# A kernel of windowed attention and a mixing MLP: its scheduler's order replaced by a written-out order, with loads and stores on two queues

## The chip, the cores and the metric

The kernel runs on one core of one Trainium2 chip. A core has five engines with a queue of instructions each: TensorE (PE, matmuls), ScalarE (ACT, activations and copies), VectorE (DVE, elementwise work), GpSimd (POOL, elementwise work and DMAs that cast) and SyncE (SP, which here issues DMAs and computes nothing). An engine takes its instructions in the order in which they stand; an instruction that has to wait for another engine waits on a semaphore, and what stands behind it waits with it. The metric is the time of the kernel on the device in microseconds (us).

## The reference

Attention over 4 batches, 8 heads, 768 positions and a head dimension of 64, in which a query sees the 128 positions up to its own and the first 4 positions (the sinks); then a block that mixes positions and channels.

```python
scores = scale * np.matmul(q, k.transpose(0, 1, 3, 2))
scores = np.where(is_sink | in_window, scores, -1000000000.0)
a = softmax(scores)                      # over keys
x = (a @ v) as [4, 768, 512]             # heads side by side
a1 = alpha1 * x + beta1
tok = np.einsum('ts,bsd->btd', w_tok, a1)
u = x + lam * tok
a2 = alpha2 * u + beta2
ch = np.maximum(a2 @ w_ch1, 0.0) @ w_ch2 # 512 -> 2048 -> 512
return u + lam * ch
```

All inputs and the output are float32.

## The kernel before

A batch goes through these steps, with tiles of 128 positions (six to a batch) and fp16 operands for TensorE:

- q and k of a pair of heads are loaded (`load_qk`, buffers `nat`), cast to fp16, transposed and put into `qkT`. In batch 0 most of them are cast by the DMA that GpSimd issues. In batches 0 and 1 TensorE transposes (`tp` tiles, L611 and L614), and ScalarE or VectorE copies the result from PSUM. In batches 2 and 3 (`b >= XB`, `XB = 2`) the DMA transposes, issued by SyncE (L630).
- `S` (L724, for some tiles with a mask bias at L719): scores of one tile of keys; ScalarE takes the exponent (`ex`, L746); VectorE or GpSimd masks the result (`mk`); `sk` and `vsp` do the sinks. `pv` (L825) multiplies with v; VectorE normalizes it into `x` (`norm`, L851). v comes by `load_v` and is cast into `vfs`.
- `xh` is the half-precision operand of the mixing: `lam * alpha1 * x` plus a constant, on GpSimd (`mul`, L869) and VectorE or GpSimd (`plus`, L872). `tok` (L956) multiplies it with the transposed w_tok; VectorE adds it to `x` (`ua`, L963), and the sum is cast to fp16 (`uc`, tile `u16`).
- `u16` is transposed into `uT`, in two halves of 384 positions: in batch 0 by TensorE (`uTp`, L997) with a scaled copy from PSUM, in the others by a DMA that SyncE issues (`uTx`, L1015) with a scaling in place (L980 on ScalarE, L982 on VectorE).
- `h` (L1036) is the first layer of the MLP, 16 tiles for each half, each four matmuls of 384 columns, and a ReLU on ScalarE or VectorE (L1042, L1044). The second layer is `ch` (L1221) in batch 0, and in batches 1 to 3 a two-level scheme with seven products instead of eight, `P1` to `P7` (L1153), with sums of halves on VectorE. The results are added to `x` and stored (`store`, L1172, and L1235).
- Weights come in early: w_tok by `load_wtok`, the four quarters of w_ch1 by DMAs on GpSimd that cast (`load_w1`), w_ch2 by `load_w` with a multiply by lam (L938).

No step is written down in the order in which it runs. Each is a task, added with `plan.add(prio, engs, fn, after, uses, ...)`: a priority, the engines that may run it and a cost in ns for each, the function that emits the instructions, the tasks it needs, the buffers it uses. There are 1,143 tasks. `Plan.run` (L132) then plays the kernel through with these costs, with a model of two DMA rings (`Rings`, L37) and fixed delays until an engine sees another's result (`SEEN`): at each step it takes the task that can start first, the higher priority first where two could start together, on the engine that would end it first, gives it free buffers, and so produces the order of every queue, the engine of every task and the buffer of every tile. The priorities come from the formulas of the code, changed at random by a list of 30 seeds (`TURNS`, L417, `shuffle`, L264). Where the model sees TensorE idle in the first 36 us it puts in matmuls on zeros (L349)[...].

All DMAs of loads and stores and all transposing DMAs are issued by SyncE; GpSimd issues those that cast, and ScalarE five small loads of parameters at the start. `gate` (L560) reads a few bytes of a quarter of w_ch1, so that SyncE waits at that point until the quarter is there. PSUM has four buffers of one bank (`d`, for everything but the scores) and two of two banks (`S`). `nat` has 8 buffers, `vnat` 4, `wst` 4, `hT` 2, `uT` and `qkT` one each.

The softmax here doesn't subtract the row's maximum and nothing guards it: scores larger than these inputs give would overflow.

## Time and profile before

| | |
|---|---|
| median of 3 runs | 257.1 us (256.68 to 257.15) |
| the profiled execution's own time | 257.06 us |
| its span, first to last instruction | 255.3 us |
| busy TensorE / VectorE / ScalarE / GpSimd | 247.4 / 190.0 / 142.6 / 88.3 us |
| HBM read, written | 29.91 MB, 6.29 MB |
| DMAs issued by SyncE for loads and stores | 101, and 34 that transpose |

The span is what the profile shows between the first and the last instruction; the execution's own time holds 1.8 us more around it. A busy TensorE is not a TensorE at its peak: matmuls are pipelined, a waiting matmul's row may be stretched, and the fillers on zeros count as busy. To see whether TensorE waits, one has to look at the steps between the starts of its matmuls. A group of the profile is named by its line; the lines of helpers (L356 is `nc.scalar.copy` in `copy`, L358 the same for the other engines) gather several tasks.

The largest loads' and stores' rows, with the median us from issue to landing:

```profile
out_dram<-x SPq DMA_DIRECT2D x21, 256.0 KB, 2.8
nat<-in_q_dram SPq DMA_DIRECT2D x13, 384.0 KB, 5.3
nat<-in_k_dram SPq DMA_DIRECT2D x13, 384.0 KB, 5.7
vnat<-in_v_dram SPq DMA_DIRECT2D x18, 256.0 KB, 5.2
```

The DMA engines are busy nearly throughout the first 70 us, and little after 170 us.

### The profile page before, as it was taken

Reading aid. Unit: us, or ns where it says so; the run is one execution under the profiler, and the core shown is the slowest. Engines: PE = TensorE matmul, PEld = TensorE weight load, DVE = VectorE, ACT = ScalarE, POOL = GpSimd, SP = SyncE. Lnnn points to the kernel's source line nnn. Section 1 sums busy time; section 2 is a strip of 40 time slices with the busy share of each in tenths; the row PEclk is TensorE's granted clock in tenths of the full one; section 3 lists DMA queues with packets and bytes.
Section 4 is the critical chain, followed back from the end, with each engine's and each line's share of the span. In section 5 each row is a group of like instructions: output and inputs, shape, how many; then the busy total and the mean of one; then the engine's idle time right before and its main releaser. Section 6 shows DMA issues by size and latency. Waiting matters only on the chain.

```text
span 255.3 us, 5519 instructions
## 1 busy us (share of the span) xinstructions
PE 247.4 (97%) x2174; PEld 160.9 (63%) x2174; DVE 190.0 (74%) x402; ACT 142.6 (56%) x236; POOL 88.3 (35%) x108
## 2 busy tenths in 40 slices
PE   8999998999999999899999999999999999999994
PEld 7754645675555544456678676558668666667883
DVE  6777998696878878578889997877789764136782
ACT  2689845989848035688971225867571125775000
POOL 7409802344445330159653460735310101000000
PEclk9999999999999999999999999999999999999999
DMA  6998999999943998599778689501000156000105
GB/s 202 195 223 292 216 230 392 373 370 218 218 73 115 186 260 190 117 205 220 155 138 182 125 191 251 85 3 21 3 0 3 59 167 146 0 0 3 63 4 185
DMA packets 86130, 38.80 MB, mean 152 GB/s; under 512 B 73540, under 2 KB 80460, under 8 KB 86104
## 3 DMA queue, kind: packets, MB, share of 16 engines
q1 hardware_dynamic: 82320, 35.14, 56.5%
q0 software_dynamic: 3744, 3.28, 8.1%
q8 instruction: 17, 0.28, 0.5%
q14 instruction: 9, 0.07, 0.1%
q10 hardware_dynamic: 40, 0.03, 0.0%
HBM read 29.91 MB, written 6.29 MB: 142 GB/s over the span
## 4 chain that ended last, share of the span: by engine, by line
PE 88%; DMA 4%; DVE 3%; POOL 1%; issue 1%; ACT 1%; POOLq 0%; ACTq 0%
PE h L1036 33%; PE P L1153 21%; PE tok L956 11%; PE ch L1221 8%; PE pv L825 5%; PE S L724 4%; DMA n<-in_q_dram 4%; DVE uT L982 1%; PE S L719 1%; PE tp L614 1%; PE pv L818 1%; POOL n L497 1%; PE wT L916 1%; ACT uT L980 1%; DVE w2f L1068 1%
## 5 line engine op out<-in xcount | busy, mean ns | idle before, releaser
L1036 PE MATMUL h<-uT,w1f 128*128 128x384 f16 x512 | 91.9, 326 | 2.7 <-DVE uT L982 1.3
L1036 PEld LDWEIGHTS <-w1f 128*128 128x128 f16 x512 | 47.3, 98 | 34.5 <-issue 5.5
L1042 ACT ACTIVATE hT<-h 128x384 f16<-128x384 f32 x99 | 48.3, 492 | 26.1 <-PE h L1036 25.6
L1153 PEld LDWEIGHTS <-hT 128*128 128x128 f16 x408 | 39.8, 98 | 6.7
L746 ACT ACTIVATE E<-S 128x1024 f16<-128x1024 f32 (+1 forms) x39 | 37.9, 1001 | 7.5 <-PE S L724 3.7
L869 POOL TENSOR_TENSOR tm<-x,la_b 128x512 f32<-128x512 f32 x18 | 26.2, 1454 | 26.3 <-DVE xh L872 19.1
L956 PE MATMUL tok<-xh,wtokT 128*128 128x512 f16 x144 | 33.4, 379 | 0.0
L356 ACT CAST u<-x 128x512 f16<-128x512 f32 x19 | 11.7, 618 | 31.2 <-DVE x L963 31.1
L1153 PE MATMUL P<-w2f,hT 128*128 128x256 f16 x216 | 25.9, 273 | 0.0
L1166 DVE TENSOR_TENSOR x<-x,P 128x256 f32<-128x256 f32 x45 | 18.3, 418 | 8.2 <-PE P L1153 7.9
L1044 DVE TENSOR_SCALAR hT<-h 128x384 f16<-128x384 f32 x29 | 15.8, 553 | 10.9 <-PE h L1036 10.5
L956 PEld LDWEIGHTS <-wtokT 128*128 128x128 f16 x144 | 14.0, 98 | 14.6
L1221 PE MATMUL ch<-w2f,hT 128*128 128x512 f16 x96 | 23.0, 379 | 0.0
L1153 PE MATMUL P<-w2s,hT 128*128 128x256 f16 x192 | 22.8, 273 | 0.0
L851 DVE TENSOR_TENSOR x<-pv,rec 128x256 f32<-128x256 f32 x48 | 20.4, 424 | 1.7
L358 POOL CAST vfs<-vnat 128x512 f16<-128x512 f32 x18 | 15.0, 840 | 16.2 <-DMA vnat<-in_v_dram 16.0
L963 DVE TENSOR_TENSOR x<-x,tok 128x512 f32<-128x512 f32 x24 | 16.2, 684 | 5.7 <-PE tok L956 5.7
L356 ACT CAST n<-nat 128x768 f16<-128x768 f32 x16 | 13.2, 829 | 10.8 <-DMA nat<-in_q_dram 8.8
L825 PEld LDWEIGHTS <-E 128*128 128x128 f16 x328 | 15.2, 97 | 6.0 <-issue 1.6
L825 PE MATMUL pv<-vfs,E 128*128 128x65 f16 x328 | 17.9, 194 | 0.0
L358 POOL CAST u<-x 128x512 f16<-128x512 f32 x5 | 3.1, 621 | 34.8 <-DVE x L963 21.1
L1221 PEld LDWEIGHTS <-hT 128*128 128x128 f16 x96 | 8.6, 98 | 9.1 <-issue 0.2
(131 smaller groups left out, 327.4 us busy)
## 6 DMA issues: line engine op xcount, KB each, us to landing
out_dram<-x SPq DMA_DIRECT2D x21, 256.0 KB, 2.8
nat<-in_q_dram SPq DMA_DIRECT2D x13, 384.0 KB, 5.3
nat<-in_k_dram SPq DMA_DIRECT2D x13, 384.0 KB, 5.7
vnat<-in_v_dram SPq DMA_DIRECT2D x18, 256.0 KB, 5.2
wst_w<-in_moe_w_ch_dram SPq DMA_DIRECT2D x8, 512.0 KB, 7.4
wtn<-in_moe_w_tok_dram SPq DMA_DIRECT2D x6, 384.0 KB, 4.7
w1f<-in_moe_w_ch_dram POOLq DMA_DIRECT2D x4, 512.0 KB, 11.1
v<-in_v_dram SPq DMA_DIRECT2D x12, 128.0 KB, 6.4
```

Of the source, the lines that this page charges most:

```text
L356: nc.scalar.copy(o, i)
L358: engine[e].tensor_copy(o, i)
L746: nc.scalar.activation(eT.t, pS.t[:, :, 0 : n * w].rearrange("p e (i w) -> p e i w", i=n), AF.Exp, scale=scale)
L825: nc.tensor.matmul(po.t[:, hl, :], eT.t[:, e_, off + i, c : c + P], vf[j][:, h, :], start=(r < 2 and n == 0), stop=(n == len(parts) - 1 an ...
L851: nc.vector.tensor_mul(bx.t[:, 4 * G : 4 * G + 4, :], po.t[:, :, 0:D], rec.t.to_broadcast([P, 4, D]))
L869: engine[e].tensor_mul(bt.t, bx.t.rearrange("p h d -> p (h d)"), la1_b)
L956: nc.tensor.matmul(pt.t, wtokT[:, si, ti * P : (ti + 1) * P], hs[si].t, start=(si == 0), stop=(si == NR - 1))
L1036: nc.tensor.matmul(ph.t, w1f[:, c, fi * P : (fi + 1) * P], bu.t[:, c, chk * NTOK : (chk + 1) * NTOK], start=(c == 0), stop=(c == NC - 1))
L1042: nc.scalar.activation(bh.t[:, fi, :], ph.t, AF.Relu)
L1153: nc.tensor.matmul(pc.t, hh[:, nt * P : (nt + 1) * P], w(fi), start=(first and n_ == 0), stop=(n_ == HF - 1), skip_group_check=True)
L1166: nc.vector.tensor_add(row(bx)[:, cols], row(bx)[:, cols], pc.t)
L1221: nc.tensor.matmul(pc.t, bh.t[:, fi, nt * P : (nt + 1) * P], w2f[:, fi, :], start=(fi == 0), stop=(fi == NF - 1))
```

## The change

The priorities, the model and the seeds go. Four literals take their place: `ORDER` (the 1,143 task numbers in the order in which they are emitted), `ENGINES` (one digit for each task: 0 ScalarE, 1 VectorE, 2 TensorE, 3 GpSimd, 4 SyncE), `HOMES` (one hexadecimal digit for each tile: its buffer) and `IDLES` (where the matmuls on zeros stand, in which PSUM buffer and how many: 101 of them, 106 before). `emit` goes through them. The tasks, what they need and what they compute are the same; the costs and priorities that are still handed to `add` are no longer read.

Loads of q, k and v of batches 1 to 3, of w_tok and w_ch2, and the stores may now be issued by ScalarE too: 25 of the 135 DMAs that were SyncE's are, 8 of q or k, 9 of v and 8 stores. The transposing DMAs stay on SyncE. `gates` has a tile of its own instead of a place in a `pt` buffer.

In number of tasks, VectorE has 336 (330 before), ScalarE 230 (229), GpSimd 108 (90), SyncE 110 (135), TensorE 359 as before. Of the 128 ReLUs, ScalarE has 81 (99 before) and VectorE 47 (29); of the 24 casts to `u16`, ScalarE 13 (19) and GpSimd 11 (5); of the 16 scalings of w_ch2, VectorE 11 (15) and GpSimd 5 (1).

```diff
-    def run(self, prio):
...
-    def emit(self, turns):
-
-        prio = [t.prio for t in self.tasks]
-        for seed in turns:
-            prio = shuffle(prio, seed)
-        for t, e, start, stop, idle in self.run(prio):
-            t.at = (e, start, stop)
+    def emit(self, order, engines, homes, idles):
+
+        own = iter(homes)
+        for t in self.tasks:
             for b in t.uses:
                 if b.home is None:
+                    b.home = int(next(own), 16)
+        fills = {i: (home, n) for i, home, n in idles}
+        for i in order:
+            t = self.tasks[i]
+            e = (ACT, DVE, PE, POOL, SP)[int(engines[i])]
+            idle = fills.get(i)
             if idle:
...
+    queue = {SP: nc.sync, ACT: nc.scalar}
...
-    gates = sb.tile([1, 32], FP16, tag="pt_1", bufs=1, name="gates")
+    gates = const.tile([1, 32], FP16, name="gates")
...
-    TURNS = (13523, 134113, 50022, 128275, 136711, 187603, 125671, 100730, 14946, 163131, 178432, 158827, 183776, 137680, 153375, 26742, 367527, 307353, 376563, 212018, 255075, 397706, 218147, 375675, 393913, 224567, 207692, 352780, 243076, 346008)
+    ORDER = (
+        26, 6, 0, 7, 9, 11, 10, 8, 18, 15, 1, 19, 45, 12, 46, 16, 47, 14, 72, 5, 48, 24, 2, 39, 49,
...
+    ENGINES = (
+        "3313134433443333444444444444444433334443131211201202021212021213030121210211201210210200"
...
+    HOMES = (
+        "5140061573001022031122213301312013300330310000011004121511643150013120133092018513113050"
...
+    IDLES = (
+        (46, 0, 54), (49, 0, 30), (90, 0, 3), (61, 3, 5), (68, 0, 2), (111, 3, 1), (88, 0, 2),
+        (166, 0, 4),
+    )
...
             done["nat", b, hp, t] = add(
-                p, {SP: 700}, lambda e: nc.sync.dma_start(
-                    bf.t.rearrange("p e (r d) -> p (e r) d", r=NR), src), [wait], [bf], lands=(96, 19.0))
+                p, {SP: 630, ACT: 600}, lambda e: queue[e].dma_start(
+                    bf.t.rearrange("p e (r d) -> p (e r) d", r=NR), src), [wait], [bf], lands=(96, 15.7))
...
         done["vn", b, r] = add(
-            p, {SP: 550}, lambda e: nc.sync.dma_start(
+            p, {SP: 570, ACT: 560}, lambda e: queue[e].dma_start(
...
         def store(p, bx, ti, cols, after):
             n_ = (cols.stop - cols.start) // 64
-            add(p, {SP: 480}, lambda e: nc.sync.dma_start(out[b, ti * P : (ti + 1) * P, cols], row(bx)[:, cols]),
+            add(p, {SP: 520, ACT: 550}, lambda e: queue[e].dma_start(out[b, ti * P : (ti + 1) * P, cols], row(bx)[:, cols]),
                 after, [bx], lands=(8, 12 * n_ if n_ == 8 else 60))
...
-    plan.emit(TURNS)
+    plan.emit(ORDER, ENGINES, HOMES, IDLES)
```

In the order of TensorE, with each run of tasks of one kind written once, the places that the prediction speaks of read as follows (`h0_0` is the first half of batch 0, `ch3` tile 3 of batch 0, a number behind x the tasks in a row):

```
before   tok0x7 uTp0x2 h0_0x4 uTp0x1 h0_0x1 uTp0x1 h0_0x4 ...
after    tok0x6 uTp0x2 tok0x1 h0_0x8 uTp0x2 h0_0x2 h0_1x9 ...

before   vsp2 ch5x2 tok1x3 ch5 tok1x3 h1_0x3 S2 sk2 h1_0x4 ...
after    vsp2 ch4 ch3 tok1x4 S2 tok1x1 ch4 ch3 tok1x1 S2 sk2 h1_0x7 ...
```

On GpSimd the start changes from `sel`, two DMAs, the identity, three DMAs, masks, `bm`, a DMA to the identity, three DMAs, masks, two DMAs, `sel`, a multiply of the parameters, `bm`, a DMA, another multiply.

## The prediction, made before the changed kernel ran

> **What bounds the kernel now.** I read the page's first two parts, then the chain of waits, then busy time by stretch, then the timeline around the two places where TensorE is short.
>
> ```profile
> span 255.3 us, 5519 instructions
> ...
> PE 247.4 (97%) x2174; PEld 160.9 (63%) x2174; DVE 190.0 (74%) x402; ACT 142.6 (56%) x236; POOL 88.3 (35%) x108
> ...
> PEclk9999999999999999999999999999999999999999
> ...
> PE 88%; DMA 4%; DVE 3%; POOL 1%; issue 1%; ACT 1%; POOLq 0%; ACTq 0%
> ```
>
> TensorE is busy 97% of the span at full clock, and the chain is TensorE for 88%. Both kernels give it the same matmuls, so only its waits can go. I sized them from the matmuls' start times: from the first matmul of a group to the first of the next, less the usual step of that kind: 0.650 us for a group of 4 in L1036 (`h`), 0.873 for 8 in L1153, 0.864 for 4 in L1221, 1.295 for 6 in L956 (`tok`), 0.24 to 0.54 for the small ones. The usual steps add up to 228.9 us. The other 26.4 lie as follows: 7.8 us up to 10 us (much of it before any input can be there), 6.3 from 10 to 30, 1.8 at 38.8 to 41.4, 2.0 at 98 to 104, 4.0 in small pieces (1.0 from 60 to 80, 1.0 from 110 to 130, 1.7 from 150 to 180 among them), nothing from 183 on, and some 4.4 after the last matmul's start.
>
> ```profile
> 0.00:17.00 17.00, 15.17 (x201) 11.41 (x201) 12.02 (x38) 9.11 (x14) 7.75 (x21) 1.00 1.04 205
> 17.00:30.40 13.40, 13.40 (x194) 7.88 (x194) 10.75 (x32) 13.08 (x22) 11.50 (x16) 1.00 1.01 253
> ...
> 38.50:42.00 3.50, 2.39 (x20) 1.39 (x19) 2.92 (x5) 2.01 (x4) 1.83 (x2) 1.00 1.06 406
> ...
> 98.00:104.00 6.00, 4.83 (x23) 2.07 (x22) 5.04 (x11) 3.06 (x5) 0.64 (x1) 1.00 0.83 179
> ```
>
> The columns are width, then PE, PEld, DVE, ACT, POOL busy with counts, clock, DMA share, GB/s. From 17 to 30.4 ScalarE is busy 13.08 of 13.40: it sets the pace there, and had 9.11 us of work done by 17. The two short rows are waits of matmuls, whose causes the timeline shows:
>
> ```profile
> 39.06 0.67 ACT L980 ACTIVATE uT<-uTp,ab 128x384 f16<-128x384 f16 x1 [1.04 <-PE uTp L997]
> ...
> 39.76 0.86 DVE L982 TENSOR_SCALAR uT<-uTp,ab 128x384 f16<-128x384 f16 x2 [0.40 <-ACT uT L980]
> ...
> 40.66 0.67 ACT L980 ACTIVATE uT<-uTp,ab 128x384 f16<-128x384 f16 x1 [0.93 <-DVE uT L982]
> ...
> 41.38 0.81 PE L1036 MATMUL h<-uT,w1f 128*128 128x384 f16 x4 [0.38 <-ACT uT L980]
> ```
>
> ```profile
> 95.97 4.02 SPq L1015 DMA_TRANSPOSE uT<-u  x3
> ...
> 101.80 0.70 ACT L980 ACTIVATE uT<-uT,ab 128x384 f16<-128x384 f16 x1
> ...
> 102.40 1.24 DVE L982 TENSOR_SCALAR uT<-uT,ab 128x384 f16<-128x384 f16 x3
> ...
> 102.83 1.35 PE L1036 MATMUL h<-uT,w1f 128*128 128x384 f16 x5 [1.07 <-DVE uT L982]
> ```
>
> In both, `h` waits for `uT`, and TensorE's order holds nothing else to fill the wait.
>
> **What the Trainium skill says.** "DMA: Bandwidth & Descriptors", section "Issuing engines are not separate DMA queues": transfers from all engines end on the same 16 DMA engines, and a second issuing engine saves only the sequencer's issue time. So I give the second queue no bandwidth. The trace has next to nothing on ScalarE's queue (40 packets), so it can't say. Section "Rules for kernel authors" of that page: two transposing streams must be kept apart, while a transpose beside ordinary DMAs needs nothing; all transposes stay on SyncE here, and I price no loss between them. "SBUF — State Buffer", section "SBUF: two separate sides": VectorE and GpSimd share a port pair that one holds for a whole instruction. The trace agrees: VectorE's scaling of w2 (L938), 0.69 us in the median, took 1.46 us at 41.13 beside GpSimd's 1.27 us multiply begun at 40.77.
>
> **The change part by part.** I call w the TensorE work, in us of the usual steps, that stands ahead of a task in an order.
>
> *Start.* Before, VectorE first casts w_tok (4.11), and the first cast of q begins at 6.39; ScalarE's first copy to `qkT` begins at 8.07. After, VectorE's first task is q's cast, and w_tok's goes to ScalarE. By the landing times of such loads (3.8 us at least from 1.27), the cast can start near 5.1 (0.76 long), six transposes follow (0.5), and ScalarE starts near 6.4, 1.7 earlier. But the last cast-on-load of k is issued by GpSimd near 9, as before (8.80), because the masks, `sel`, `bm` and a 1.2 us multiply stand ahead of it; it landed 8.2 us after issue, so near 17.1 both orders meet the same wall. Before, TensorE then had w = 5.9 behind it, after, 6.45. ScalarE's work ahead of `tok` (w = 16) is 24.9 us before and 25.2 after, by row durations. ScalarE's instructions overlap by 0.10, so of the 1.7 some 1.2 us counts at most, and the extra work and the wall take part of it. I take `tok` at 29.7 instead of 30.5: −0.8 (bounds −1.8 and +0.5).
>
> *First `uT` of batch 0.* After, the last three of six `tok` groups end differently: six `tok`, the two `uTp`, and then one more `tok` of 1.295 us before the first `h`. The four copies are two on ScalarE (0.67) and two on VectorE (0.47), side by side: 0.2 + 2 x 0.67 = 1.5 us against 1.3 us of cover. Of 1.75 us lost, 0.3 stays: −1.4 (bounds −1.7, −0.8).
>
> *tok of batch 1.* Before, the chain from the end of the third `tok` (97.0) through L963, the cast, the transposing DMA (issued 98.77, used 101.80) to the last L982 (103.65) takes 6.65 us. After, behind the last `tok` that the first half needs stand three other `tok`, two `S`, one `sk` and two `ch`: 3 x 1.295 + 2 x 0.435 + 0.333 + 2 x 0.864 = 6.8 us. The 2.0 us go (bounds −2.0, −0.8). Next late would be batch 2's first `S`, which moves from w = 86.2 to 79.9: its last transpose is issued at w = 75.7, plus 2.8 us to land, 78.7, so 1.2 us are in hand.
>
> *25 DMAs on ScalarE* (8 loads of q/k, 9 of v, 8 stores). The ones at the start on this queue took 0.51 to 0.58 us each; SP's issues of the same loads took 0.37 to 3.58 us for v, 0.37 to 2.40 for q/k. At 0.55 they are 13.8 us of ScalarE's time, and 18 of 128 ReLUs leave it for VectorE. ScalarE is idle for 44%, so the time itself is hidden; a long issue isn't, because exps and ReLUs stand behind it in order, and four PSUM buffers give TensorE about 3 x 0.65 = 1.95 us. A ring that is full is the open cost: 0 to 0.4 us each.
>
> *Moves to GpSimd.* It gets 108 tasks for 90: 100 us of work for 81, by its rows (1.2 us where VectorE needs 0.42 to 0.69). From w = 44.4 to 65 VectorE holds 22.0 us of work in 20.6; back-to-back instructions overlap by 0.083, which leaves 19.4, so it is nearly full and a port wait shows. Before, VectorE's port waits were 6.3 us in all, 3.4 of them from 40 to 80. I allow +0.5 (bounds 0, +2).
>
> *w1's fourth quarter.* `h` of batch 0 needs it from w = 27.4 instead of 43. Its load was issued at 27.58 and such loads take 11.1 us: 38.7. TensorE gets there at 29.7 + 11.4 + 0.3 = 41.4. Nothing (bounds 0, +2).
>
> *The rest.* Cost numbers, the gates' own tile and the w2 order change no instruction's length. The tail's stores stay 4.4 us behind the last matmul. I expect small waits in other places, as many as now (4.0), and add +0.5 for the pieces that a new order brings.
>
> Sum: −0.8 − 1.4 − 2.0 + 0.5 + 0.5 = −3.2. The profiled execution took 257.06 (its span and 1.8 around it), which is the median of 257.1 to within 0.1: **253.9**.
>
> **The rivals.**
> 1. The small waits go too: without the two allowances of 0.5, and with 1.6 of the 4.0 gone, 253.9 − 1.0 − 1.6 = 251.3. For it: they come from the same kind of order. Against: each of them has another cause, and ScalarE's issues are new.
> 2. Given back: VectorE in w = 38 to 65 becomes the bound, by +3 us more of port waits and late masks: 256.9. For it: the 19.4 in 20.6. Against: ScalarE has room there.
> 3. Slower: ScalarE's loads block what stands behind them. In 54.7 to 69.2 SP needed 7.66 us for five v loads, 1.5 each, and 5.6 for four of q/k. If ScalarE sees the same, each of 17 loads costs TensorE what exceeds the buffers' 1.95 us and what was already late, 0.36 in the mean: 17 x 0.36 = 6.1 in place of the two allowances, so 252.9 + 6.1 = 259.0. It decides from 0.25 us for each load, which eats the 4.2. Against: ScalarE's ring is its own, and seldom has two loads in a row.
> 4. That the change doesn't do what it says is excluded: the program's order shows the 25 DMAs on ScalarE.
>
> **How the numbers follow.** Main case 0.52 (its own range 252.3 to 255.6), rival 1 0.13, rival 2 0.13, rival 3 0.22. What can be told from no change is 0.2%, 0.5 us. Rival 2's spread gives 0.07 within that, 0.03 on either side. Faster 0.52 + 0.13 + 0.03 = 0.68, same 0.07, slower 0.25. The range reaches from rival 1 to rival 3: 251.0 to 258.8.
>
> **What would show it.** Right: the first `tok` starts before 30.2; `h` of batch 0 loses under 0.6 us behind `uTp`; no wait over 0.5 us before batch 1's `h`; ScalarE's DMA issues stay near 0.6 us. Wrong: ACT waits or issues above 2 us followed by TensorE waits of `h` or `S`; TensorE waiting for w1f near 41 us; `S` of batch 2 waiting for a transpose; a `tok` start later than 31.

## The result, and the profile after

The changed kernel takes 264.62 us in the median of four runs (263.71 to 266.96), the kernel before 256.93 (256.68 to 257.15) on the same chip: a ratio of 1.0313, 95% interval 1.0246 to 1.0381. It is 3% slower. The prediction was 253.9, with a range of 251.0 to 258.8: a gain was forecast and a loss came. A later series of four runs of the same kernel gave 263.09 (262.42 to 266.52), ratio 1.0223 (1.0196 to 1.0249; a run over 1.5% above the fastest of its kernel is left out of such a ratio, so this one rests on three). Its times spread over 3 to 4 us, those of the kernel before over 0.5 to 1.2.

The page of the profiled execution (263.71 us), first and fourth part:

```profile
span 262.0 us, 5519 instructions
...
PE 248.2 (95%) x2169; PEld 160.7 (61%) x2169; DVE 202.3 (77%) x406; ACT 129.6 (49%) x214; POOL 107.6 (41%) x128
...
PE 72%; DVE 15%; SPq 5%; DMA 5%; issue 3%; DVEq 0%
```

TensorE does the same work in a span that is 6.7 us longer. The chain that ended last was TensorE for 88% and is now for 72%; VectorE has 15% of it (3% before), and SyncE's queue and transfers 10% (4%). The waits of TensorE in the same execution (us in total, times, the longest):

```profile
PE tp L507 <- DVE n L157: 2.3, 2, 1.7
PE S L617 <- DMA qkT<-n: 1.4, 1, 1.4
PE P L1046 <- DVE x L1059: 1.4, 3, 0.8
PE uTp L890 <- DVE hT L937: 1.2, 1, 1.2
PE pv L718 <- DVE x L744: 1.2, 1, 1.2
```

None of these pairs was among the waits of the kernel before, of which the largest were `h` behind `uT`. Lines of the changed kernel: L507 are the transposes of the start, L617 is the first `S` of batch 2, L1046 `P`, L890 `uTp`, L718 `pv`; in the kernels of the experiments, after2 apart, they stand a line higher. The two stretches of the prediction, in the busy times by window (columns as there), of the changed kernel:

```profile
38.50:42.00 3.50, 3.50 (x27) 2.03 (x26) 3.41 (x7) 1.36 (x3) 0.00 (x0) 1.00 1.03 386
...
98.00:104.00 6.00, 4.57 (x27) 1.93 (x26) 2.06 (x3) 2.62 (x4) 1.79 (x3) 1.00 1.17 182
```

At 38.5 to 42 TensorE is now never idle: that wait is gone. At 98 to 104 it has 4.57 us of work where it had 4.83: that wait has only changed its place, and TensorE now stands at `S`.

To see where the time went, I compare the two traces at equal work. The lag at w is the start of the matmul that has w us of TensorE's usual steps ahead of it, less the same for the kernel before, both from the first instruction. Its growth is what a stretch of the order loses. "Second trace" is the run after2, the changed kernel once more.

| stretch of w | what is in it | predicted | lost, first trace | second trace |
|---|---|---|---|---|
| 0 to 20 | start, up to the `tok` of batch 0 | -0.8 | +1.76 | +1.13 |
| 20 to 28 | first `uTp` and `h` of batch 0 | -1.4 | -1.61 | -1.06 |
| 28 to 32 | `uTp` of the second half | 0 | +1.54 | +0.42 |
| 32 to 74.7 | `h`, `ch` of batch 0 with `pv` of batch 1 | +0.5 | +1.55 | +1.51 |
| 74.7 to 100 | `tok` of batch 1, first `S` of batch 2, `h` | -2.0 | -0.27 | +0.84 |
| 100 to 220 | batches 1 to 3 | +0.5 for all that is left | +1.27 | +1.26 |
| 220 to the last matmul | last `P` of batch 3 | in the same | +1.30 | +1.29 |
| behind the start of the last matmul | last sums and stores | 0 | +1.16 | +0.81 |
| sum | | -3.2 | +6.70 | +6.20 |

The sums are the differences of the spans: 262.0 and 261.5 against 255.3. Only one of three predicted gains came. The stretches that lost add up to 8.6 us in the first trace; 5.3 of them (28 to 32, and everything from 100 on) lie at places for which the prediction had nothing but one common term of 0.5.

### The profile page after: what moved, and what is told of

Same layout as the page of the kernel before. It is cut to its first block, busy times and chain, and to the rows that moved or that the text cites. A ratio compares the mean times of both kernels' runs of the same rounds, so it can differ in the third digit from the quotient of the medians.

```text
span 262.0 us, 5519 instructions
## 1 busy us (share of the span) xinstructions
PE 248.2 (95%) x2169; PEld 160.7 (61%) x2169; DVE 202.3 (77%) x406; ACT 129.6 (49%) x214; POOL 107.6 (41%) x128
## 4 chain that ended last, share of the span: by engine, by line
PE 72%; DVE 15%; SPq 5%; DMA 5%; issue 3%; DVEq 0%
PE h L929 28%; PE P L1046 18%; PE tok L849 9%; SPq L523 4%; PE pv L718 4%; PE S L617 3%; DVE w2f L831 3%; DMA nat<-in_k_dram 3%; DMA qkT<-n 2%; DVE E L654 2%; PE ch L1114 2%; DVE x L1059 2%; PE S L612 2%; PE tp L507 1%; DVE hT L937 1%
## 5 line engine op out<-in xcount | busy, mean ns | idle before, releaser
L929 PE MATMUL h<-uT,w1f 128*128 128x384 f16 x512 | 89.4, 326 | 0.2 <-DVE x L1059 0.2
L935 ACT ACTIVATE hT<-h 128x384 f16<-128x384 f32 x81 | 37.8, 494 | 37.3 <-PE h L929 37.0
L1046 PEld LDWEIGHTS <-hT 128*128 128x128 f16 x408 | 39.5, 98 | 8.9 <-issue 2.1
L937 DVE TENSOR_SCALAR hT<-h 128x384 f16<-128x384 f32 x47 | 25.6, 554 | 20.0 <-PE h L929 19.1
L762 POOL TENSOR_TENSOR tm<-x,la_b 128x512 f32<-128x512 f32 x18 | 24.6, 1368 | 29.9 <-DVE x L744 18.7
L1046 PE MATMUL P<-w2f,hT 128*128 128x256 f16 x216 | 26.5, 273 | 0.6 <-DVE x L1059 0.6
L1046 PE MATMUL P<-w2s,hT 128*128 128x256 f16 x192 | 22.8, 272 | 0.8 <-DVE x L1059 0.8
L849 PEld LDWEIGHTS <-wtokT 128*128 128x128 f16 x144 | 13.8, 98 | 15.1 <-issue 0.4
L157 POOL CAST u<-x 128x512 f16<-128x512 f32 x11 | 8.4, 773 | 34.6 <-DVE x L856 28.8
L1059 DVE TENSOR_TENSOR x<-x,P 128x256 f32<-128x256 f32 x45 | 17.9, 415 | 5.8 <-PE P L1046 5.3
L155 ACT CAST u<-x 128x512 f16<-128x512 f32 x13 | 7.9, 617 | 28.4 <-DVE x L856 25.6
L744 DVE TENSOR_TENSOR x<-pv,rec 128x256 f32<-128x256 f32 x48 | 20.4, 425 | 1.7
L1085 POOL TENSOR_TENSOR x<-x,pt 128x512 f32<-128x512 f32 x4 | 5.7, 1419 | 36.3 <-DVE pt L1077 32.8
L155 ACT CAST n<-nat 128x768 f16<-128x768 f32 x20 | 16.3, 829 | 6.9 <-DMA nat<-in_k_dram 6.4
L718 PEld LDWEIGHTS <-E 128*128 128x128 f16 x328 | 15.1, 98 | 6.9 <-DVE x L744 1.7
L718 PE MATMUL pv<-vfs,E 128*128 128x65 f16 x328 | 17.7, 194 | 1.4 <-DVE x L744 1.2
L579 POOL TENSOR_SCALAR_AFFINE_SELECT E<-E 128x512 f16<-128x512 f16 x18 | 12.8, 735 | 14.3 <-ACT E L639 14.3
```

The source lines that it names most:

```text
L155: nc.scalar.copy(o, i)
L718: nc.tensor.matmul(po.t[:, hl, :], eT.t[:, e_, off + i, c : c + P], vf[j][:, h, :], start=(r < 2 and n == 0), stop=(n == len(parts) - 1 an ...
L744: nc.vector.tensor_mul(bx.t[:, 4 * G : 4 * G + 4, :], po.t[:, :, 0:D], rec.t.to_broadcast([P, 4, D]))
L762: engine[e].tensor_mul(bt.t, bx.t.rearrange("p h d -> p (h d)"), la1_b)
L849: nc.tensor.matmul(pt.t, wtokT[:, si, ti * P : (ti + 1) * P], hs[si].t, start=(si == 0), stop=(si == NR - 1))
L929: nc.tensor.matmul(ph.t, w1f[:, c, fi * P : (fi + 1) * P], bu.t[:, c, chk * NTOK : (chk + 1) * NTOK], start=(c == 0), stop=(c == NC - 1))
```

## Experiments

All kernels are written-out orders with the literals of the changed kernel, so an edit moves a task's number in `ORDER` or its digit in `ENGINES`, and nothing else. The numbers are those of the tasks. Three theories at first:

- Port: GpSimd's extra work makes VectorE's instructions longer, and these are what TensorE waits for. (Port is the pair of SBUF ports that VectorE and GpSimd share, of which the prediction speaks.)
- Queue: the 25 DMAs on ScalarE delay the transfers that TensorE waits for, or what stands behind them on ScalarE.
- Order: the places in TensorE's own order leave no slack, whatever the other engines do.

"Lengthened" means below: by at least 0.15 us over what the same instruction takes when it is quick; these excesses of VectorE add up to 7.6 us before and 18.5 after.

### One part alone

a_pool_back and a_dma_sp take one part out of the changed kernel; b_pool and b_dma_act put one into the kernel before, whose own order was written out for it. In the listings below, a line with - is what stood there and a line with + what stands there instead; spaces and slashes keep cases apart.

```diff
 ENGINES, the 32 tasks that the change moved to GpSimd: a_pool_back
-3 (GpSimd)
+1 or 0 (VectorE or ScalarE, as before)
 ENGINES, the 25 DMAs that the change moved to ScalarE: a_dma_sp
-0 (ScalarE)
+4 (SyncE)
 The same two groups in the kernel before: b_pool and b_dma_act
-1 or 0 / 4
+3       / 0
```

> The changed order with the 32 tasks that went to GpSimd put back on the engine they had before (23 on VectorE, 9 on ScalarE); the order, the buffers and the 25 DMAs on ScalarE stay. Port theory (GpSimd's extra work holds the port pair and stretches VectorE, 18.5 us of stretches against 7.6): 260 to 261, and the stretches fall below 10 us. Queue theory (the DMAs on ScalarE delay the transposing ones): 264, no change. Order theory (the places in TensorE's order are the cause): 264, or more, since VectorE gets 15 us more work.

> The changed order with its 25 DMAs put back on SyncE's queue at the same places. Queue theory: the transposing DMAs of qkT land in about 2.8 us again instead of 4.5, the wait before batch 2's first S (1.7 us) goes, and the time falls to 262 to 263. Port theory: 264, no change. Order theory: 264, or more, because SyncE now stands in front of busy buffers.

> The order of before, written out, with the same 25 DMAs on ScalarE and nothing else changed. Queue theory: 259 to 260. Port theory and order theory: 257, within 0.5 us.

> The order of before, written out, with the same 32 tasks on GpSimd and nothing else changed. Port theory: 261 to 263, with VectorE's stretches up by some 8 us. Queue theory and order theory: 257 to 258, since VectorE loses about 16 us of work and GpSimd has room.

Measured, with the kernel before at 256.86: a_pool_back 272.23 (ratio 1.0593, 1.0535 to 1.0651), a_dma_sp 267.94 (1.0445, 1.0393 to 1.0496), b_dma_act 262.0 (1.0184, 1.0146 to 1.0223), b_pool 261.42 (1.0163, 1.0135 to 1.0192). Put into the kernel before, each part costs about 5 us; taken out of the changed kernel, where it was to bring something back, it costs 3 (a_dma_sp) and 8 us (a_pool_back) more than the first series. So neither part alone is the cause, and the new order needs the placement that it came with. By the times alone the order theory had a_pool_back and a_dma_sp right (264 or more), the port theory b_pool, and nobody b_dma_act, which is 2 us above what the queue theory allowed. The traces say more than the times:

- a_pool_back has 8.9 us of lengthening left and is the slowest. The tasks themselves then stand on VectorE and ScalarE, and TensorE waits 2.7 us at an `h` of batch 0 and 4.5 us at the first `S` of batch 2. But its lag hardly grows from w = 156 to 228: the changed kernel's waits at the tail are gone.
- b_pool has about as much lengthening as the changed kernel (17.9 us), and its lag is 2.87 us at w = 6.4, where VectorE waits for the two multiplies by lam that GpSimd now does (1.27 us each, 0.68 on VectorE): a copy of 128 x 8 values, 0.3 us in e_bpool below, takes 3.46 beside them. From there to the end the lag grows by 0.85 us, and 0.7 us more lie outside the span. Some 15 us of lengthening behind the start cost little, since this order has slack there.
- b_dma_act loses 3.4 us at one place, w = 25 to 28 (its lag goes from -0.33 to 3.06). Its timeline of ScalarE, and what ScalarE waited for in that window:

```profile
40.32 0.67 ACT L872 ACTIVATE uT<-uTp,ab 128x384 f16<-128x384 f16 x1 [0.93 <-DVE uT L874]
44.46 0.41 ACTq L396 DMA_DIRECT2D nat<-in_q_dram  x1
44.96 0.62 ACT L155 CAST u<-x 128x512 f16<-128x512 f32 x1 [3.97 <-DMA wst_w<-in_moe_w_ch_dram]
```

The issue of the load takes 0.41 us, but ScalarE stood in front of it from 41.0 to 44.46 until a load of w_ch2, which SyncE had issued before, had landed. The cast to `u16` behind it needed none of this; the next ReLU stood behind the cast, and TensorE waited 2.7 us for it at a `uTp`. This is rival 3's mechanism, as one wait of 4 us and not as a little for each load.

The trace also shows why: the 140 DMAs that ScalarE and SyncE issue take eight semaphores in turn (17 or 18 DMAs each), and the program has an engine wait until the DMA that used a semaphore last has landed before it issues the next one with it. This load's semaphore belonged to the load of w_ch2 that SyncE had issued at 36.24; its landing is recorded at 44.38, and the issue follows at 44.46. The two waits of ScalarE in c_port below end in the same way (landed 43.06 and 44.41, issued 43.08 and 44.43). So against what the prediction held against rival 3, ScalarE's ring is not wholly its own: a slow load of SyncE can hold it.

a_dma_sp and b_dma_act together say when transposes land late. The transposes of keys land in 2.8 us in the median in the kernel before and also in b_dma_act, in 3.1 in a_dma_sp, and in 4.5 in the changed kernel: it takes both the new order, which puts loads beside them, and the second queue. TensorE waits 1.0 us at the first `S` of batch 2 in a_dma_sp, as the queue theory said (1.4 in the changed kernel's first trace, 2.6 in its second). But with one queue VectorE waits 4.1 us for a store that SyncE issues late, behind transposes, and TensorE 3.3 us at an `h` behind it.

### Four local waits mended, and the two named gains alone

In the first trace, VectorE instructions that TensorE soon waits for are lengthened at four places. The plainest is at `pv` of batch 1, in the timeline of the changed kernel:

```profile
72.90 1.65 POOL L762 TENSOR_TENSOR tm<-x,la_b 128x512 f32<-128x512 f32 x1 [6.27 <-DVE x L744]
...
73.33 1.50 DVE L961 TENSOR_TENSOR w2s<-w2f,w2s 128x512 f16<-128x512 f16 x1
...
76.74 0.30 PE L718 MATMUL pv<-vfs,E 128*128 128x65 f16 x4 [1.18 <-DVE x L744]
```

L961 sums halves of w2, which nobody needs for a long while; it takes 1.50 us beside GpSimd's multiply where 0.42 is usual. A second such sum (0.82) and then the `norm` (L744) that frees the PSUM buffer for the next `pv` stand behind it. This multiply is none of the 32 tasks that moved: GpSimd has all 18 of them in the kernel before too. In a_pool_back, where the 32 are back, the same pair meets, and TensorE waits 1.13 us at the same `pv`:

```profile
76.64 1.65 POOL L761 TENSOR_TENSOR tm<-x,la_b 128x512 f32<-128x512 f32 x1 [7.08 <-DVE x L743]
...
77.07 1.50 DVE L960 TENSOR_TENSOR w2s<-w2f,w2s 128x512 f16<-128x512 f16 x1
```

So what brought this wait is the new order of VectorE, which puts the sums there, and not GpSimd's extra work.

```diff
 c_port: ENGINES, tasks 39, 41 (lam multiplies, 39 also a few places later), 1116 (sum of batch 3)
-3 (GpSimd)
+1 (VectorE)
 c_port: ORDER on VectorE
-238, 182, 181, 296, 294, 290, 247, 248, 242
+238, 296, 294, 290, 247, 248, 182, 181, 242
-392, 356, 345, 414, 416, 429
+392, 414, 416, 429, 356, 345
 c_s2: ORDER on TensorE (653 is the first S of batch 2, 480 a tok)
-653, 480, 332, 326
+480, 332, 653, 326
 d_two: the kernel before, ORDER on TensorE (229 a tok, 338 a ch, 504 an h)
-217, 229, 226, 220, 223, 259, 235, 237, 239, 241, 244, 246, 257
+217, 226, 220, 223, 229, 259, 235, 237, 239, 244, 257, 241, 246
-464, 338, 472, 476, 480, 504, 488, 490
+464, 472, 476, 480, 338, 488, 490, 504
```

Exponents, ReLUs and sums that follow from a moved task move with it on their engines. c_all has the edits of c_port and c_s2.

> The changed kernel with its order, queues and placement, except at four places where a VectorE instruction that TensorE soon waits for ran up to three times as long beside a GpSimd instruction: the two lam multiplies of the start and one sum of the last group go back to VectorE, and four VectorE instructions (the scalings of w2 before the second uTp, two half sums of w2 before pv of batch 1) are put a few places later. Port theory (stretches cost only where the order leaves no slack): the lag behind the kernel before falls by 1.0 at the start, 1.4 at w = 32, 1.2 at w = 58 and 0.7 to 1.0 at the tail, in all 3 to 4.5 us: 260 to 261.5. Order theory (whatever is mended, the next late task takes its place): less than 1.5 us in all, 263 to 264.5. Queue theory (ScalarE's loads are the cost): no change, since no DMA is moved.

> The changed kernel with one move: the first S of batch 2, with its two exponents, stands behind the last tok of batch 1 and the ch that follows, instead of before them (2.2 us of TensorE work later). If the late transposes of batch 2's keys cost only this wait of 1.7 us, the lag at w = 85 to 90 falls by 1.3 to 1.7 and the time to 263.0 to 263.3. If the next task was as late (the h of batch 1 behind uT, or S's later users), under 0.5 is won: 264.2 to 264.7. Queue theory adds nothing here: the transposes still land late beside ScalarE's loads.

> Both of the above together. If the losses are local and add up: 258.5 to 260, a lag behind the kernel before of under 3.5 us at the end. If they hide one another, it is no faster than the better of the two by more than 0.5 us.

> The kernel before, its own order written out, with its own engines and queues, and only the two rearrangements for which the prediction had named a gain: one tok of batch 0 behind the two uTp of the first half (the uTp of the second half behind five h instead of three and four), and one ch behind the last tok of batch 1, ahead of h. If the prediction sized these two places right (1.4 and 2.0 us) and only the other parts of the change cost time, 253.6 to 254.6. If such waits come back elsewhere whatever is done, 256 to 258. Port and Queue theories say nothing here, since no task changes its engine and no DMA its queue.

Measured, with the kernel before at 256.69: c_port 264.38 (260.32 to 265.03, too wide for a ratio), c_s2 262.32 (1.0211, 1.019 to 1.0231), c_all 262.35 (1.0222, 1.0201 to 1.0242), d_two 256.41 (0.9987, 0.9975 to 0.9999). By place:

- At w = 54 to 58 c_port loses 0.03 instead of 1.39, and at 220 to 224.4 nothing instead of 0.99; the second gives 0.83 back at the next `P`. So lengthened instructions are what TensorE waited for at these two places. At the first the edit only changes VectorE's order; at the second it takes a task off GpSimd, and the net gain is 0.16.
- At w = 28 to 32 it holds its loss (1.45), and at 24.8 to 28 it loses 0.69 where the changed kernel won 1.11: ScalarE was idle for 4.7 us around the issues of two loads of batch 1, in front of which it waited as in b_dma_act. In the first trace of the changed kernel the first of these loads found its way free; in the second trace ScalarE was idle for 3.3 us there, and TensorE waited 0.6.
- c_s2 takes the wait of 1.7 us at `S` away, and 1.6 us come back at `h`, which waits for the transpose of `u16`. Its gain against the first trace is nearly all in the start (next paragraph).
- d_two gains 0.8 at the first named place and gives it back by w = 32, to ReLUs that stand behind four copies on ScalarE; at the second it gains 0.3.

The start is partly chance. VectorE's second cast and GpSimd's multiply in the first trace of the changed kernel, then in c_s2, which has the same start:

```profile
8.51 1.26 POOL L1164 TENSOR_TENSOR la_b<-la_b,lam_r 128x512 f32<-128x512 f32 x1 [0.53 <-DMA la_b<-in_moe_alpha_dram]
8.53 1.66 DVE L157 CAST n<-nat 128x768 f16<-128x768 f32 x1 [2.26 <-DMA nat<-in_k_dram]
```

```profile
8.69 0.56 DVE L157 CAST n<-nat 128x768 f16<-128x768 f32 x1 [3.04 <-DMA nat<-in_k_dram]
...
8.71 1.67 POOL L1163 TENSOR_TENSOR la_b<-la_b,lam_r 128x512 f32<-128x512 f32 x1 [1.35 <-DMA la_b<-in_moe_alpha_dram]
```

Whichever begins 0.02 us sooner is quick, and the other waits for it: the cast takes 1.66 us or 0.56. The Trainium skill states this in "SBUF — State Buffer", section "SBUF: two separate sides": VectorE and GpSimd share a pair of ports as a lock for a whole instruction. Here TensorE's next transpose stands behind the cast, so 1.1 us of the kernel hang on 0.02. Landing times add to this: kernels that keep the start of the kernel before have a lag at w = 6.4 from -0.4 (e_bpool) to +0.7 us (e_two).

### Blocking, traffic, and the two gains set more closely

e_q3 is c_all with three loads of batch 1 (174 to 176) back on SyncE and one copy (86) from ScalarE to VectorE. e_q3l puts five loads behind `h` of batch 1. e_two sets d_two's edits closer. e_bpool is b_pool with the two multiplies left on VectorE. (c_all's load waited for a load of w_ch2, not for a quarter of w1, as the expectation of e_q3 has it.)

```diff
 e_q3: ENGINES, tasks 174, 175, 176 / 86
-0 / 0
+4 / 1
 e_q3l: loads 626, 879, 624, 882, 880, place in ORDER
-around 653 to 651, ahead of h of batch 1
+behind 498, its second h
 e_two: ORDER on TensorE, then on VectorE, against d_two
-239, 244, 257, 241, 246, 261
+239, 244, 241, 257, 246, 261
-481, 339, 468, 470, 471, 346
+481, 468, 470, 471, 339, 346
```

> c_all (the changed kernel with the four places mended and the first S of batch 2 later) with two edits more. The three loads of q and k of batch 1 that ScalarE issues between the copies to uT and the ReLUs of batch 0 go back to SyncE, at the same place in the order: in c_all ScalarE stood 4.7 us in front of them, waiting for a quarter of w1, and h waited 1.8 us for the ReLU behind. And one copy to PSUM's reader for w_tok (0.7 us) ahead of the first tok goes from ScalarE to VectorE. Blocking theory (a DMA that has to wait holds up ScalarE): the lag behind the kernel before at w = 28 to 32 falls from 2.4 to between -0.8 and 0.5, and at w = 16 by 0.5 to 0.7, if ScalarE sets the pace there: 259.5 to 260.5. Order theory: what follows is late anyway, and less than 1 us comes of both.

> e_q3, and the five loads of v of batch 2 and of q and k of batch 3 that stand in the order between the last tok of batch 1 and its h (four on ScalarE, one on SyncE) are issued behind the second h. If these loads' traffic is what makes the transposes of keys and of u land in 4 to 5 us there instead of 2.8, they land in about 3, the wait of h of batch 1 (1.3 us in c_all) falls under 0.5, and the time is 0.8 to 1.5 us under that of e_q3. If the transposes are slow because they stand one behind the other on SyncE's queue, nothing changes.

> The kernel before with the two rearrangements of d_two, set more closely: the uTp of the second half follow one h later than in the kernel before instead of behind five in a row, and the sum behind the moved ch stands behind the scalings of uT on VectorE instead of between them. In d_two the first place won 0.4 and gave back 0.8 to ReLUs that stood behind four copies on ScalarE, and the second won 0.3, with 0.7 us of this sum in its wait. Expected 255.2 to 256.0. If the waits only move, 256.3 to 256.8.

> The kernel before, its own order, with 30 of the 32 tasks on GpSimd as in the changed kernel, and the two lam multiplies of the start left on VectorE. In b_pool, with all 32, 2.9 of the 3.7 us were lost before w = 6.4, where VectorE waited for these two multiplies in front of a sum for the sink scores. If that is their whole effect, 257.0 to 258.0, with VectorE's instructions lengthened beside GpSimd by some 17 us in all and nearly nothing of it on the path. If Port theory holds wherever instructions are lengthened, 260 or more.

Measured, with the kernel before at 256.66: e_q3 262.33 (1.0205, 1.0176 to 1.0234), e_q3l 265.18 (1.0327, 1.0312 to 1.0341), **e_two 255.33 (0.9957, 0.9943 to 0.997)**, e_bpool 257.81 (1.005, 1.0037 to 1.0063).

- e_bpool is where it was expected: 30 of the 32 moves to GpSimd cost 1.1 us, of which its lag shows 0.8 behind the start. Of the 17 us of lengthening that were expected 11.1 showed.
- e_two beats both kernels, by 1.3 us the one before. Busy times of e_two, then of the kernel before, around its two places:

```profile
34.00:50.00 16.00, 15.60 (x105) 8.91 (x104) 12.75 (x23) 11.49 (x22) 3.45 (x4) 1.00 1.10 340
96.00:106.00 10.00, 9.66 (x56) 4.42 (x55) 6.65 (x17) 6.54 (x11) 0.64 (x1) 1.00 0.85 175
```

```profile
34.00:50.00 16.00, 14.89 (x98) 8.49 (x97) 12.63 (x21) 11.20 (x22) 3.52 (x4) 1.00 1.10 346
96.00:106.00 10.00, 8.83 (x51) 4.01 (x49) 6.92 (x16) 5.54 (x10) 0.64 (x1) 1.00 0.77 166
```

  TensorE gets 0.7 and 0.8 us more done in the same stretches. By the lag, each place wins 0.86 us, of which the second gives back 0.2 by w = 100.
- e_q3 wins 1.1 us from w = 24.8 to 28, where c_all lost 0.6: with ScalarE free of the loads the gain is there again. It then loses 3.8 us up to w = 36: the scalings of w2 that c_port had put later now stand in front of a copy to `uT` (1.75 us of one of them, beside GpSimd). That is the edit's own doing. Its other edit took 0.7 us off ScalarE ahead of `tok`, and the loss from w = 12 to 16 went up, from 0.95 to 1.43: ScalarE, busy there nearly all the time, does not set that pace.
- e_q3l tells what the traffic does. Transfers issued from 94 to 107 us, median us to landing, in e_q3 and then in e_q3l:

```profile
vnat<-in_v_dram ACTq DMA_DIRECT2D x2, 256.0 KB, 4.6
...
qkT<-n SPq DMA_TRANSPOSE x4, 3.8
uT<-u SPq DMA_TRANSPOSE x3, 6.3
```

```profile
uT<-u SPq DMA_TRANSPOSE x5, 3.5
qkT<-n SPq DMA_TRANSPOSE x3, 3.2
```

  These medians rest on few landings, since the trace keeps only some: 6.3 is one transpose of `u`, issued at 100.1 beside the loads; 3.5 is two, 2.44 us for one issued at 99.6, before any of the loads, and 4.49 for one issued at 105.5, just ahead of them. With the loads away the transposes land sooner, and the wait of `h` behind them (1.2 us) is gone. But the loads then stand on ScalarE among the ReLUs of that `h`, and one of them waits for an earlier transfer:

```profile
107.04 1.63 ACTq L406 DMA_DIRECT2D vnat<-in_v_dram  x1
110.10 0.37 ACTq L400 DMA_DIRECT2D nat<-in_k_dram  x1
110.52 0.49 ACT L934 ACTIVATE hT<-h 128x384 f16<-128x384 f32 x1 [3.52 <-DMA uT<-u]
```

  TensorE waits 3.4 us for PSUM behind it.

### Everything mended at once

f_beta tests VectorE as the pace ahead of the first `tok`. f_fix joins all mends; f_fix2 and f_fix3 each take away the largest wait that the one before had made. after2 is the changed kernel, unchanged. g_store moves two stores.

```diff
 f_beta: 39 and 41 on VectorE, and ORDER on VectorE (149 is the beta of x)
-159, 149, 155, 151, 89, 167, 163
+159, 155, 151, 89, 167, 149, 163
 f_fix: f_beta; c_port's edits, with 182 and 181 behind 272 and 288; c_s2's edit;
 174 to 176 on SyncE; the loads on SyncE behind the last transpose of batch 1
+479, 626, 624, 879, 880, 882
 f_fix2: f_fix; load 627 and two casts on ScalarE (901, 903) placed anew
+479, 626, 624, 627, 879, 880, 882
+549, 901, 547, 903
 f_fix3: f_fix2; casts 899 and 897 behind 705 and 905, transpose 898 behind 904
 g_store: the changed kernel, stores 864 (ScalarE) and 873 (SyncE) of batch 2
-the first of them 13 us before the end, behind 1127
+behind 1085, near 239 us
```

> The changed kernel with the two lam multiplies of the start on VectorE, as in the kernel before, and with one VectorE task later: the scaled copy plus beta of the first tile of x (0.74 us, not needed before the sum behind the first tok) stands behind the last norms of batch 0 instead of ahead of three of them. The changed kernel loses 0.95 us between w = 12 and w = 16. Pace of VectorE theory: the norms, and the wT transpose that waits for the PSUM buffer of one of them, come 0.7 us earlier, and the lag growth from 12 to 16 falls from 0.95 to 0.1 to 0.4; 262.0 to 263.0 with the start's chance collision gone. Pace of ScalarE theory (it was busy 14.8 of 15 us there): the growth stays at 0.9, 263.2 to 264.2.

> The changed kernel mended at every place where a cause was found: the two edits of f_beta; the three loads of q and k of batch 1 from ScalarE back to SyncE; the two scalings of w2 that took 1.5 to 1.75 us beside GpSimd behind the copies to uT that they held up; two half sums of w2 behind the norms of batch 1; the first S of batch 2 later; the five loads of batch 2 and 3 that slowed the transposes of u behind those transposes, on SyncE, where they hold up no ReLU; one sum of the last group on VectorE. 29 of the 32 tasks stay on GpSimd, 18 of the 25 DMAs on ScalarE, and all other places in the order. If the loss is the sum of these local waits, the lag at w = 32, 58, 90 and 228 falls from 1.7, 3.0, 3.4 and 5.5 to about -0.8, -0.7, -1.5 and 1, and the time to 256 to 258.5. If it comes from placement as a whole (GpSimd's share, two queues), or waits only move, 260 or more.

> f_fix with its one large new wait taken away. There, TensorE waited 5.3 us in batch 1's h, because ScalarE stood in front of a cast of keys of batch 3 whose load had been put later, with a ReLU and an exponent behind it. Here that cast and the next one stand behind later ReLUs on ScalarE, and one load of v of batch 2 goes ahead of those of batch 3 on SyncE. f_fix was level with the kernel before up to w = 90 (a lag of 0.06 us, of which 0.5 from the start). If the losses are local waits that can be mended one by one, the lag at w = 100 is 0 to 1 instead of 6.4 and at the end 1.5 to 2.5: 257.5 to 259.5. If the waits move on whatever is done, 262 or more.

> f_fix2 with its new wait taken away in turn. f_fix2 was 0.4 us behind the kernel before at w = 100 and then lost 3.8 us, 2.2 of them at one h, because ScalarE stood for 2.5 us in front of a cast of keys of batch 3 whose load had landed late, with ReLUs behind it. Here this cast stands behind the ReLUs and exponents that it held up, and one cast and one transpose that follow from it are put later too. Local theory: the lag stays near 0.5 to 1 until w = 127, and ends at 2 to 3.5, as the changed kernel's own waits behind w = 127 (2.5 us) are not touched: 258.5 to 260. If the waits move on whatever is done: 262 or more.

> The changed kernel itself once more, for a second trace. Places where the order leaves no slack should show in both traces: the growth of the lag before the first tok (0.95), at the uTp of batch 0 (1.5), at pv of batch 1 (1.4) and at the tail (1.0 and 0.3). Places that hang on when a transfer lands or on which of two instructions begins first should differ: the start (between 0.9 and 2.0 behind the kernel before, as VectorE's second cast falls beside GpSimd's multiply or not), and the first S of batch 2 (a wait of 1.2 to 3.1 us in the runs of this order). 262.5 to 267.

> The changed kernel with one edit at its end. Two 256 KB stores of batch 2 (one on ScalarE's queue, one on SyncE's), whose sums were done at 216.1 and 218.8 us, are issued only at 257.0 and 253.8 us, among the last stores of batch 3; here they are issued near 239. The changed kernel's span ends 5.5 us behind the start of its last matmul, that of the kernel before 4.4 us, and 2.1 MB go out in its last 8 us instead of 1.2. If these two stores' traffic is the cause, this stretch falls to 4.3 to 4.8 us and nothing ahead of it changes; the whole time, which spreads by 3 us for other reasons, is 0.7 to 1.2 lower than without the edit. If the stretch is set by the last sums on VectorE, it stays at 5.3 or more.

Measured, with the kernel before at 256.81 to 256.96: f_beta 265.86 (ratio 1.0311, 1.0249 to 1.0373), f_fix 267.06 (1.0434, 1.0364 to 1.0504), f_fix2 263.33 (1.0241, 1.0207 to 1.0274), f_fix3 264.91 (1.0302, 1.0271 to 1.0333), after2 263.09 as above, g_store 261.85 (1.0178, 1.0142 to 1.0213). The lag by place:

| w | changed | after2 | f_beta | f_fix | f_fix2 | f_fix3 | e_two |
|---|---|---|---|---|---|---|---|
| 12 | 0.81 | 0.18 | -0.23 | 0.51 | -0.14 | -0.58 | 0.65 |
| 20 | 1.76 | 1.13 | 0.78 | 1.57 | 0.87 | 0.62 | 0.65 |
| 32 | 1.69 | 0.49 | 0.76 | 0.10 | -0.61 | -0.85 | -0.21 |
| 58 | 3.04 | 1.81 | 2.31 | 0.79 | 0.80 | -0.61 | -0.25 |
| 90 | 3.40 | 3.27 | 5.49 | 0.06 | 0.09 | -1.33 | -1.01 |
| 100 | 2.97 | 2.84 | 5.06 | 6.37 | 0.41 | -0.90 | -0.89 |
| 120 | 3.05 | 2.92 | 5.14 | 6.45 | 4.25 | 4.85 | -0.88 |
| 228 | 5.54 | 5.39 | 7.58 | 8.44 | 6.25 | 6.87 | -0.87 |

- Up to w = 90 the mends hold. From w = 12 the changed kernel loses 2.6 us to there, f_fix, f_fix2 and f_fix3 -0.5, 0.2 and -0.8. In f_fix the transposes of `u` of batch 1 whose landings the trace keeps land in 2.4 us, where the changed kernel's took 6.1 and 4.7.
- Behind it f_fix, f_fix2 and f_fix3 lose 8.4, 6.2 and 8.2 us up to w = 228, the changed kernel 2.1; each has its own reasons for the 4 to 6 us more: the loads that were put off for the transposes land late, casts on ScalarE stand in front of them, and ReLUs behind the casts (5.3 us in f_fix, 2.2 in f_fix2; in f_fix3 a late cast keeps a buffer that VectorE's sums of halves for `P` need, 2.3 us). Expected were 256 to 258.5, 257.5 to 259.5 and 258.5 to 260; none came below 262, and from 260 or 262 on the expectations had said that waits only move on. So the losses up to w = 90 can be mended locally; that the sum of local waits explains the whole loss is not shown, and whether the order as a whole can be had level with the kernel before stays open.
- f_beta speaks for neither theory: from w = 12 to 20 it loses 1.01, the changed kernel 0.95. What costs this 0.95 in both traces stays open. Its first `S` of batch 2 waited 3.1 us for transposes, 1.7 in the first trace, 2.9 in the second: here the time of the kernel hangs on landing times, which may be part of its spread.
- g_store's span ends 4.6 us behind the start of its last matmul, the changed kernel's 5.5 and 5.2, the kernel before's 4.4. The stores were the cause of that: the last store of all is issued 0.8 us behind the start of TensorE's last matmul in both, and lands 2.73 us later in the changed kernel and 1.80 in g_store (1.72 in the kernel before). The large stores issued from 254 to 262 us in the changed kernel and from 255 to its end at 263.3 in g_store, with us to landing:

```profile
out_dram<-x ACTq DMA_DIRECT2D x3, 256.0 KB, 2.9
out_dram<-x SPq DMA_DIRECT2D x5, 128.0 KB, 2.7
```

```profile
out_dram<-x SPq DMA_DIRECT2D x5, 128.0 KB, 1.8
out_dram<-x ACTq DMA_DIRECT2D x2, 256.0 KB, 2.3
```

  The same five small stores land in 1.8 us instead of 2.7 when the two large ones of batch 2, ready since 216 and 219 us, have gone out before.

## Why the prediction was wrong, step by step

The prediction failed at three of its steps: at the start (a gain of 0.8, measured a loss of 1.1 to 1.8), at the 2.8 us that it gave a transpose to land (measured 5.07 and 5.84), and at the +0.5 for all places that it had not looked at (measured 3.4 to 3.7 from w = 100 on alone).

*Start, -0.8; measured +1.76 and +1.13 at w = 20.* The cast of q did come earlier (5.61 instead of 6.39) and ScalarE's first copy too (6.87 instead of 8.07, 1.2 earlier where the prediction had 1.7). The failed step is the next one, that a part of this head start counts up to the first `tok` ("so of the 1.7 some 1.2 us counts at most"): nothing of it lasts, because the next transposes need k, whose cast began at 8.53 after and 8.70 before, in all kernels run between 8.1 and 9.4: the load of k lands then in any order. ScalarE had nothing to do from 8.4 to 10.8. The first `tok` of the changed kernel began at 32.1, not 29.7; the prediction had named a start later than 31 as a sign of being wrong. On top come the two multiplies on GpSimd (up to 1.1 us, by chance) and 0.95 us between w = 12 and 16 whose cause wasn't found.

*First `uT` of batch 0, -1.4.* Right, in the mechanism too: -1.61 and -1.06, with TensorE busy throughout the window from 38.5 to 42. Alone in the kernel before's order it is worth 0.86 (e_two). What the prediction lacked is the next wait in the row, `uTp` of the second half, +1.54 and +0.42: VectorE's scalings of w2 (1.50 and 1.75 us beside GpSimd) in front of the ReLU that frees its PSUM buffer, or ScalarE in front of a load.

*tok of batch 1, -2.0.* The failed step is "its last transpose is issued at w = 75.7, plus 2.8 us to land, 78.7, so 1.2 us are in hand". The 2.8 were taken from the kernel before. The transposes of keys before, then after:

```profile
qkT<-n SPq DMA_TRANSPOSE x16, 2.8
```

```profile
qkT<-n SPq DMA_TRANSPOSE x16, 4.5
```

The last one ahead of that `S` was issued near w = 76, as predicted, and took 5.07 us (5.84 in the second trace), because loads of batch 2 and 3 now run beside it; in a_dma_sp, with these loads on SyncE, it took 2.74. The prediction had read "a transpose next to ordinary DMAs needs nothing" ("DMA: Bandwidth & Descriptors", section "Rules for kernel authors") as a price; it speaks of waits that correctness needs, not of time. This place was named in the prediction as what would make it wrong. In the kernel before's own order and traffic the rearrangement is worth 0.6 to 0.9 (e_two), not 2.0; what keeps the rest from coming there was not traced.

*25 DMAs on ScalarE, 0.* The issue time was below what was allowed: 10.4 us in all instead of 13.8, 0.34 to 0.92 us each. Missing were three other costs: the traffic (above), the waits of a DMA in front of ScalarE's other work (idle times of ScalarE around such issues of 4.0 us in b_dma_act, 4.7 in c_port, 3.5 in e_q3l, 3.3 in after2), and the two late stores (0.6 to 0.95 at the end), where the prediction had said that "the tail's stores stay 4.4 us behind the last matmul". The prediction's own sum for rival 3, 259.0, already lay outside the range that was to reach to it. Rival 3 had the mechanism, but spread it evenly over 17 loads; it comes as single waits, and in the first trace of the changed kernel as none that TensorE waited for.

*Moves to GpSimd, +0.5 with bounds 0 and 2.* In the kernel before's order 1.1 us without the lam multiplies (e_bpool). In the changed order lengthened instructions cost more, at places the prediction did not look at: 1.39 at `pv` of batch 1 (beside a multiply that GpSimd had before), 0.99 at the last `P` (0.16 when mended, as the next wait came up), part of the 1.54 at the second `uTp`. The step looked at VectorE's fill from w = 44 to 65 and not at which single instruction has TensorE close behind it.

*w1's fourth quarter, 0.* Right: no matmul waited for it in the first trace.

*The rest, +0.5.* The largest error: w = 100 to the end lost 3.7 and 3.4 us by itself. 1.3 of it is in the last `P`, 0.99 of that behind VectorE's lengthened sum, 0.6 to 0.95 are the stores, and 1.3 from w = 100 to 220 were not tried; these lie near w = 143 to 156, and a_pool_back and a_dma_sp lose 1.2 us or more there too, so neither part of the placement brings them alone. A new order of 1,143 tasks was priced at three known places, with a constant for all others.

## What to carry over

A written-out order belongs to its placement: moving DMAs or elementwise work to another engine changes durations and landing times in many places, so times that were measured in the old kernel (2.8 us for a transpose, 0.42 for a sum) must not be counted on in the new one. Price a DMA on a computing engine by what stands behind it and by what it may have to wait for, not by its issue time. And when a whole order changes, look for every place where a wait's releaser has a single short instruction of margin, or rearrange only the two places that the profile names: that was worth 0.4% here (e_two, 0.3 to 0.6%), where the full change cost 2 to 3%.

## What the runs showed of the hardware

- Transposing DMAs land later beside loads of another queue: those of `u` of batch 1 took 6.1 and 4.7 us in the changed kernel and 2.4 in f_fix, where the loads come behind them; those of keys 4.5 us in the median, 3.1 with the same loads on SyncE's queue (a_dma_sp).
- Two instructions of VectorE and GpSimd that begin within 0.02 us of each other take 1.66 and 1.26 us or 0.56 and 1.67, by which of them is first.
- A load's issue on ScalarE takes 0.4 us, but ScalarE stood 3.5 us in front of one (b_dma_act), until a transfer that SyncE had issued and whose semaphore it shares had landed. The program's 140 DMAs of these two engines share eight semaphores.
- Some 15 us of lengthening on VectorE behind the start cost b_pool 0.85 us there, while one copy that took 3.46 us instead of 0.3 cost it 2.9 at the start: a lengthened instruction costs only where nothing else covers it.
- Two 256 KB stores left to the end made the last 128 KB store land in 2.73 us instead of 1.80 (g_store).
